# A gated delta-net kernel on one core: one 64x64 Gram product per unit, the first group inverted on VectorE, a new order by chunk

## The chip, the core and the metric

The kernel runs on one NeuronCore of a Trainium2 chip. The metric is device microseconds of one execution; the kernel before was run three times, and the median counts. TensorE (PE) multiplies, VectorE (DVE), ScalarE (ACT) and GpSimd (POOL) work element by element, and SyncE (SP) issues the DMAs. [...]

## The reference

Four batches with 8 heads each hold 768 tokens of 48 features, in float32. The first part is a recurrence over the tokens, the second a gated convolution on its output.

```python
def _attn_ref(q, k, v, beta):
    k_n = k / (np.linalg.norm(k, axis=-1, keepdims=True) + 1e-06)
    state = np.zeros((B, H, D, D))
    for t in range(S):
        y[:, :, t] = np.einsum('bhd,bhde->bhe', q[:, :, t], state)
        v_old = np.einsum('bhde,bhd->bhe', state, kt)
        state = state + bt[:, :, :, None] * np.einsum('bhd,bhe->bhde', kt, vt - v_old)

def _moe_ref(x, w_val, conv_w, w_out):      # x: the four batches, 768 tokens, 384 features
    for k in range(5): gate_pre += conv_w[k] * xp[:, k:k + S, :]
    gate = 1.0 / (1.0 + np.exp(-gate_pre))
    return (gate * (x @ w_val)) @ w_out
```

## The kernel before

The tokens are cut into 12 chunks of 64, two chunks to a group, and each chunk is done for all 32 pairs of batch and head at once. Only the state goes from chunk to chunk.

For a **group**, `prep` makes the inverse of a triangular matrix for each of its 64 units (a pair of batch and head in a chunk; 64 tokens, cut into two blocks of T=32). `gram` multiplies the keys with keys and queries: per head four streams (two row halves by two column halves of the array), and in each two products of 32 rows, with a moving operand of up to 96 columns. Its PSUM result is copied by ACT into GD (`gk`: per row block the diagonal 32x32 block and the lower left one) and multiplied by a mask on DVE into AQ (`ga`). DVE then transposes the diagonal blocks so that units lie on partitions (`trans_in` into TLP), takes norms and coefficients (`coef`), and inverts: 8x8 blocks row by row (`row`), pairs of them to 16x16 (`mergez8`, `merget8`). From there two ways lead on. Group 0 (`FAST`) packs the 16x16 inverses, transposes them back and builds the 32x32 inverses on PE with `p1`, `p2`, `p3` and ACT copies. All other groups go on on DVE with `zmul`, `zred`, `tmul`, `tred`, and transpose the result twice, into BD (`trans_t`) and into TNA (`trans_n`). Last, `lev1` and `lev2` on PE with ACT copies (`zevac`, `tevac`) put the off-diagonal 32x32 block into BD.

For a **chunk**, `chain` does `estep` (keys by state) and `esum`, `qstep`, `ustep` (inverse times ES, the chunk's update), `sstep` (new state, accumulated in the PSUM banks SPS) and `ystep` (output); `flip` transposes the output into X. `moe` follows: `halo` carries the last four tokens over, `conv` does the first `nt` of the five taps of the convolution on PE, `tap` the others on DVE, then `sig`, `val`, `gate`, `outp` and the output's DMA. The taps on PE are 2 in chunks 0 to 5 and 1 in chunks 6 to 11 (`TAPS`, `PTAP`).

The two 384x384 weights and the convolution's come as float64 and are made float32 by five steps of ACT and DVE (`f64_bits`), one of ACT (`f64_low`) and two of POOL (`f64_join`), over two staging buffers that are the tiles GT and OS.

What sets the order: all operations are added to a `Plan` with an engine, an estimated cost and their inputs and outputs. The plan gives each a rank (the length of what follows it, plus a number of the table `BIAS` by kind and group), and lays them out greedily by estimated time. Six PSUM banks are handed out on the way. Where it thinks PE idle or little used it puts in `keep_warm`, a product of zeros (128x128 by 128) into an unused part of SPS. The result is a fixed list for each engine. Loads go through SP in the plan's order, each behind a one-element DMA (PACE) that reads what the load two before it has written, so that two are in flight.

Of the kernel before, what the change touches and what calls it, by code (L numbers as in the profile page):

```python
# [21 lines left out]
KW = 5 * T  # L22
# [3 lines left out]
NBANK = 6  # L26
BIAS = {
    'LB': -1138.3, ('LB', 0): 7.4, 'LK0': 530.9, ('LK0', 0): -481.0, 'LKQ': 1110.0, ('LKQ', 0): -19.7,
    ('LKQ', 1): 156.3, ('LKQ', 2): 217.7, ('LKQ', 3): -442.9, ('LKQ', 4): -892.6, ('LKQ', 5): -89.1, 'LKT': -576.7,
    ('LKT', 0): -196.1, ('LKT', 1): -334.4, ('LKT', 2): 445.2, ('LKT', 3): -254.0, ('LKT', 4): 323.2,  # L30
# [30 lines left out]
    ('outp', 0): -290.2, ('outp', 1): -378.5, ('outp', 2): 246.7, ('outp', 3): 155.7, ('outp', 4): 185.1,
    ('outp', 5): 238.1, 'p1': -8.9, ('p1', 0): -189.4, 'p2': -61.8, 'p2evac': -59.9, ('p2evac', 0): 440.8,
    ('p2', 0): -32.9, 'p3': 33.8, 'p3evac': 482.3, ('p3evac', 0): 751.7, ('p3', 0): -185.1, 'pack': -348.7,
    ('pack', 0): 465.1, 'qstep': 59.2, ('qstep', 0): 391.9, ('qstep', 1): 424.1, ('qstep', 2): -186.8,
    ('qstep', 3): -217.3, ('qstep', 4): -80.2, ('qstep', 5): -107.5, 'row': -870.9, ('row', 0): 33.6,
# [948 lines left out]
```

## Time and profile before

| | |
|---|---|
| three runs | 342.68, 342.65, 339.18 us; median 342.65 |
| profiled execution | 342.16 us, of which the program's span is 340.4 |
| PE busy | 294.2 us (86%) in 8370 matmuls |
| DVE busy | 265.4 us (78%) in 655 instructions |
| ACT, POOL busy | 195.9 us (58%), 17.6 us (5%) |
| DMA | 34.58 MB, 102 GB/s over the span |

A float32 product of the program is two matmuls in the profile, each with its own weight load; transposes are one. [...] The chain of waits gives PE 45% of the span, DVE 21%, ACT 15%, and 10% to "issue", time in which an engine waited for nothing that the profile shows. The profile begins with setup and the first groups' inversions, and the first `ustep` starts at 66.66 us; from about 110 us on PE is busy nearly throughout.

### The profile page before, as it was taken

The page shows a single profiled execution, that of the slowest core. Times are in us where ns is not written, and L with a number is a line of the kernel's source. Part 1 is how long each engine was busy: PE and PEld are TensorE (multiplying, and loading weights), DVE is VectorE, ACT ScalarE, POOL GpSimd, SP SyncE. Part 2 cuts the span into 40 slices and gives each one's busy share as a digit, 9 for nine tenths or more (in the row PEclk, how much of TensorE's full clock was granted, in tenths as well). Part 3 has the DMA queues.
Part 4 walks back from the last instruction along what each step waited for, and adds up shares of the span by engine and source line. Part 5 has one row for each costly group of instructions (what it writes and reads, how often), then busy time and mean ns, then how long its engine had stood idle before and what let it go on. Part 6 is the DMA issues. An engine that isn't in the chain of part 4 may idle for free.

```text
span 340.4 us, 18482 instructions
## 1 busy us (share of the span) xinstructions
PE 294.2 (86%) x8370; PEld 236.6 (70%) x8370; DVE 265.4 (78%) x655; ACT 195.9 (58%) x569; POOL 17.6 (5%) x31
## 2 busy tenths in 40 slices
PE   5898544977859898988996997998999999999994
PEld 4797544876647776875875885877866787687862
DVE  5569869895257999998999866999999899827430
ACT  4211759999545965357955478616599351873321
POOL 0000022322200000000000000000000000000000
PEclk9589855969678999999999589999999999999999
DMA  4885666131612527060147104345221301300213
GB/s 149 271 251 155 193 187 187 52 91 58 202 53 81 171 54 233 19 196 11 50 81 257 58 4 157 62 125 162 58 65 26 98 4 25 73 4 2 49 23 69
DMA packets 12379, 34.58 MB, mean 102 GB/s; under 512 B 1933, under 2 KB 5133, under 8 KB 12301
## 3 DMA queue, kind: packets, MB, share of 16 engines
q1 hardware_dynamic: 12300, 33.41, 33.4%
q8 instruction: 65, 1.06, 1.3%
q14 instruction: 14, 0.11, 0.1%
HBM read 28.69 MB, written 4.72 MB: 98 GB/s over the span
## 4 chain that ended last, share of the span: by engine, by line
PE 45%; DVE 21%; ACT 15%; issue 10%; DMA 7%; SPq 0%; POOL 0%; DVEq 0%; ACTq 0%
PE PB L907 8%; PE SPS L958 6%; PE PB L915 5%; PE PB L892 5%; ACT VN L348 5%; PE PB L484 5%; DMA KQ<-in_kq_dram 5%; DVE GT L898 4%; PE PB L801 2%; ACT BD L348 2%; PE PB L833 2%; DVE ZT L606 2%; ACT US L348 2%; DVE PR L599 2%; PE PB L851 2%
## 5 line engine op out<-in xcount | busy, mean ns | idle before, releaser
L907 PE MATMUL PB<-X,WV 128*128 128x256 f32 x216 | 52.5, 388 | 1.5 <-DVE GT L910 1.0
L915 PE MATMUL PB<-WO,GT 128*128 128x384 f32 x144 | 50.6, 495 | 0.1
L348 ACT ACTIVATE VN<-VN,NRM 128x48 f32<-128x48 f32 x192 | 45.1, 326 | 2.2 <-DMA PACE<-VN 2.0
L907 PEld LDWEIGHTS PB<-X,WV 128*128 128x128 f32 x216 | 39.8, 191 | 8.5 <-DVE GT L910 1.2
L898 DVE SCALAR_TENSOR_TENSOR GT<-X,CW,GT 128x256 f32<-128x256 f32 x90 | 38.7, 478 | 0.1
L958 PE MATMUL SPS<-ZW 128*128 128x128 f32 x214 | 35.1, 319 | 3.0 <-DVE SPS L400 2.8
L915 PEld LDWEIGHTS PB<-WO,GT 128*128 128x128 f32 x144 | 26.3, 190 | 15.5 <-DVE GT L910 0.3
L484 PE MATMUL PB<-KQ 48*32 48x96 f32 (+2 forms) x1536 | 26.6, 263 | 11.7 <-issue 9.2
L958 PEld LDWEIGHTS SPS<-ZW 128*128 128x128 f32 x214 | 31.2, 224 | 4.4 <-DVE SPS L400 2.8
L484 PEld LDWEIGHTS PB<-KQ 48*32 48x32 f32 x1536 | 21.3, 113 | 16.0 <-issue 11.9
L892 PE MATMUL PB<-X,CD 128*128 128x256 f32 x108 | 32.0, 432 | 0.1
L348 ACT ACTIVATE OS<-PB 128x384 f32<-128x384 f32 x24 | 11.6, 487 | 34.4 <-PE PB L915 33.1
L910 DVE TENSOR_TENSOR GT<-PB,GT 128x256 f32<-128x256 f32 x36 | 14.9, 417 | 20.5 <-PE PB L907 20.5
L494 DVE TENSOR_TENSOR AQ<-PB,MASK 128x256 f32<-128x256 f32 x48 | 19.2, 418 | 12.7 <-ACT GD L348 12.6
L898 DVE SCALAR_TENSOR_TENSOR GT<-X,CW,PB 128x256 f32<-128x256 f32 x36 | 16.6, 475 | 13.8 <-PE PB L892 8.7
L348 ACT ACTIVATE US<-PB 64x384 f32<-64x384 f32 (+1 forms) x36 | 17.5, 486 | 16.8 <-PE PB L812 9.2
L348 ACT ACTIVATE GD<-PB 128x256 f32<-128x256 f32 x48 | 15.6, 381 | 18.8 <-PE PB L484 18.4
L348 ACT ACTIVATE BD<-PB 32x256 f32<-32x256 f32 (+1 forms) x50 | 19.1, 383 | 8.7 <-PE PB L697 5.8
L892 PEld LDWEIGHTS PB<-X,CD 128*128 128x128 f32 x108 | 21.0, 210 | 3.6 <-DVE GT L898 0.3
L902 ACT ACTIVATE GT<-GT 128x256 f32<-128x256 f32 x36 | 13.6, 413 | 15.3 <-DVE GT L898 15.2
L841 PEld LDWEIGHTS PB<-US,AQ 64*64 64x64 f32 x768 | 14.3, 146 | 9.7 <-ACT US L348 7.1
L348 ACT ACTIVATE ZS<-PB 32x256 f32<-32x256 f32 x48 | 17.9, 373 | 4.1 <-PE PB L686 3.1
(117 smaller groups left out, 481.9 us busy)
## 6 DMA issues: line engine op xcount, KB each, us to landing
KQ<-in_kq_dram SPq DMA_DIRECT2D x24, 640.0 KB, 5.0
VN<-in_vt_dram SPq DMA_DIRECT2D x12, 384.0 KB, 3.5
KT<-in_kt_dram SPq DMA_DIRECT2D x12, 384.0 KB, 3.2
out_dram<-OS SPq DMA_DIRECT2D x48, 96.0 KB, 2.2
BD<-in_k_dram SPq DMA_DIRECT2D x2, 512.0 KB
OS<-in_w_val_dram SPq DMA_DIRECT2D x2, 384.0 KB, 4.0
GT<-in_w_out_dram SPq DMA_DIRECT2D x2, 384.0 KB
PACE<-KQ SPq DMA_DIRECT2D x24, 0.0 KB
```

The source lines that it names most:

```text
L348: A.activation(out=out, in_=in_, func=AF.Copy, **kw)
L484: PE.matmul(o, w, y, start=True, stop=True, tile_position=(64 * r, q))
L494: V.tensor_tensor(out=AQ[c % NAQ][:, r, 4 * i:4 * i + 4, :].rearrange("p h (n t) -> p h n t", t=T), in0=gview(c, i, r, part)[:, :, 0:3:2, ...
L599: V.tensor_tensor(out=PR[:, 0:64 * n].rearrange("p (k i j) -> p k i j", k=4, i=16), op=ALU.mult, in0=tl4[:, 1, :, 0, 4 * kb:16].unsqueeze( ...
L841: PE.matmul(bank("y", c, r)[a:a + C, D * h:D * h + D], aq[64 * t:64 * t + C, r, h, :], us[64 * t:64 * t + C, r, h, :], start=c == 0 and h ...
L892: PE.matmul(p, CD[:, m, k], x[:, m, :, k:k + C], start=(k == 0), stop=(k == nt - 1))
L898: V.scalar_tensor_tensor(out=GT[m], in0=x[:, m, :, k:k + C], scalar=CW[:, m, k:k + 1], in1=csum(m) if k == nt else GT[m], op0=ALU.mult, op ...
L902: A.activation(out=GT[m], in_=csum(m) if nt == KS else GT[m], func=AF.Sigmoid)
L907: PE.matmul(p, WV[:, k, 128 * m:128 * m + 128], xs[:, k], start=(k == 0), stop=(k == NKX - 1))
L910: V.tensor_tensor(out=GT[m], in0=bank("v", c, m)[:, 0:B * C].rearrange("p (b t) -> p b t", t=C), in1=GT[m], op=ALU.mult)
L915: PE.matmul(bank("o", c, i)[:, 0:DM], GT[k][:, 2 * i:2 * i + 2, :].rearrange("p b t -> p (b t)"), WO[:, k, :], start=(k == 0), stop=(k == ...
L958: PE.matmul(SPS[0][:, 384:512], ZW, ZW, start=False, stop=True, skip_group_check=True)
```

## The change

- `FAST` and its functions are gone (`pack`, `trans_x`, `split`, `p1`, `wsum`, `p2`, `p2evac`, `p3`, `p3evac`, and the constants they need): group 0 takes the way of the others on DVE.
- `gram` does one product per stream and head: 64 stationary columns, and 128 moving columns (64 for group 0, whose keys alone come first from K0). The queries no longer stand twice in the load, so a KQ load has 128x1024 elements, not 128x1280. The blocks of the result lie otherwise: a new `place`, two ACT copies of 32 partitions by 1024 elements per group, brings the two upper diagonal blocks to where `trans_in` reads them.
- TNA is laid out [128, T, NU]: `trans_n` writes it contiguously, and `lev2` reads its stationary operand with a stride of 32 elements.
- `halo` runs on ACT instead of POOL.
- The taps on PE are 3 in chunks 0 to 5 (2 before); chunks 6 to 11 keep 1.
- `BIAS` is a new table, by chunk where it was by group (`plan.part = c`), and the planner's costs and columns are changed; with them the lists of all engines. The program's products on PE: `gram` 896 before and 448 now, `p1` to `p3` 320 and 0, `conv` 54 and 72, `keep_warm` 107 and 181; the others as before.

```diff
-KW = 5 * T
+KW = 4 * T
...
-FAST = (0,)
-TAPS = 2
-PTAP = {6: 1, 7: 1, 8: 1, 9: 1, 10: 1, 11: 1}
+TAPS = 3
+PTAP = {2: 3, 6: 1, 7: 1, 8: 1, 9: 1, 10: 1, 11: 1}
...
-TICK_COLS = 1450.0
+TICK_COLS = 1270.0
...
-    TNA = sb.tile([128, NU, T], F32, name="TNA")
+    TNA = sb.tile([128, T, NU], F32, name="TNA")
...
     def gram(c, i, part):
-        x = KQ[c % NKQ]
-        for j in range(4):
-            h = 4 * i + j
-            for k in range(2):
-                for r, t in STREAMS:
-                    q = 64 * t + 32 * k
-                    o = bank("g", c, i, r, part)[q:q + 32, 96 * j:96 * j + 96].rearrange("p (n t) -> p n t", t=T)
-                    if part == "K":
-                        y = K0[64 * r:64 * r + D, c, t ^ r, h, :]
-                        w, y = y[:, k * T:k * T + T], y.rearrange("p (n t) -> p n t", t=T)
-                        y, o = y if k else y[:, 0:1].to_broadcast([D, 2, T]), o[:, 0:2, :]
-                    else:
-                        y = x[64 * r:64 * r + D, t ^ r, h, :]
-                        w, y = y[:, (2 + k) * T:(3 + k) * T], y.rearrange("p (n t) -> p n t", t=T)
-                        n, m = {"": ((0, 5, 2), (0, 3, 1)), "Q": ((0, 5, 4), (0, 3, 2))}[part] if k == 0 else \
-                            {"": ((2, 5, 1), (0, 3, 1)), "Q": ((4, 5, 1), (2, 3, 1))}[part]
-                        y, o = y[:, n[0]:n[1]:n[2], :], o[:, m[0]:m[1]:m[2], :]
-                    PE.matmul(o, w, y, start=True, stop=True, tile_position=(64 * r, q))
-
-    def gview(*key):
-        return bank("g", *key)[:, 0:384].rearrange("p (h n t) -> p h n t", n=3, t=T)
+        for h in range(4 * i, 4 * i + 4):
+            for r, t in STREAMS:
+                y = (K0[:, c] if part == "K" else KQ[c % NKQ])[64 * r:64 * r + D, t ^ r, h, :]
+                n = y.shape[-1] if part == "" else C
+                PE.matmul(bank("g", c, i, r, part)[64 * t:64 * t + C, n * (h % 4):n * (h % 4) + n], y[:, 0:C],
+                          y[:, C:] if part == "Q" else y, start=True, stop=True, tile_position=(64 * r, 64 * t))
+
+    def gview(c, i, r, part):
+        n = C if part else 2 * C
+        return bank("g", c, i, r, part)[:, 0:4 * n].rearrange("p (h n) -> p h n", n=n)
 
     def gk(c, i, r, part):
         u = 16 * (c % 2) + 8 * r + 4 * i
-        copy(GD[c // 2 % 2][:, u:u + 4, :].rearrange("p h (n t) -> p h n t", t=T), gview(c, i, r, part)[:, :, 0:2, :])
+        copy(GD[c // 2 % 2][:, u:u + 4, :], gview(c, i, r, part)[:, :, 0:C])
 
     def ga(c, i, r, part):
-        V.tensor_tensor(out=AQ[c % NAQ][:, r, 4 * i:4 * i + 4, :].rearrange("p h (n t) -> p h n t", t=T),
-                        in0=gview(c, i, r, part)[:, :, 0:3:2, :], op=ALU.mult,
-                        in1=MASK.rearrange("p (n t) -> p n t", t=T).unsqueeze(1).to_broadcast([128, 4, 2, T]))
+        V.tensor_tensor(out=AQ[c % NAQ][:, r, 4 * i:4 * i + 4, :], in0=gview(c, i, r, part)[:, :, 0 if part else C:],
+                        in1=MASK.unsqueeze(1).to_broadcast([128, 4, C]), op=ALU.mult)
...
+        def place(q):
+            copy(GD[gb][q:q + 32, :, T:], GD[gb][q:q + 32, :, 0:T])
...
-            V.transpose(out=TNA.rearrange("p u k -> p k u"), in_=tf)
...
+            V.transpose(out=TNA, in_=tf)
...
-                    PE.matmul(bank("o2", g, i)[to:to + 32, T * j:T * j + T], TNA[q:q + 32, 16 * i + j, :], ZS[i][q:q + 32, j, :],
+                    PE.matmul(bank("o2", g, i)[to:to + 32, T * j:T * j + T], TNA[q:q + 32, :, 16 * i + j], ZS[i][q:q + 32, j, :],
...
+            plan.part = c
             loads(c)
             plan_gram(c, "Q" if g == 0 else "")
         for c in (2 * g, 2 * g + 1):
+            plan.part = c
             tokens(c)
...
-        add("DVE", 1.87, trans_in, r=GDT[0] + GDT[1], w=["TL"])
+        for q in (0, 64):
+            add("ACT", 1.05, place, (q,), r=GDT[0] + GDT[1], w=[("GDp", gb, q)])
+        add("DVE", 1.87, trans_in, r=GDT[0] + GDT[1] + [("GDp", gb, q) for q in (0, 64)], w=["TL"])
...
-        if g in FAST:
-            for b in range(2):
-                add("ACT", 0.5, pack, (b,), r=["TT"], w=["PR"])
-            add("DVE", 0.63, trans_x, w=["PR"])
-            add("ACT", 1.15, split, (1,), r=["PR", "MHI"], w=["RH"])
-            add("ACT", 1.15, split, (0,), r=["PR", "TRQ"], w=["TZ"])
-            for i in range(2):
-                add("PE", 1.1, p1, (i,), cols=512, size=256, r=["RH"] + GDT[i], w=[("wp", i)], take=[("w", g, i)])
...
-            add("DVE", 1.87, trans_n, r=["TT"] + tm, w=[("TNA", i, q) for i in range(2) for q in (0, 64)])
...
+        add("DVE", 1.2, trans_n, r=["TT"] + tm, w=[("TNA", i, q) for i in range(2) for q in (0, 64)])
...
-            G.tensor_copy(out=XB[(c + 1) % 3][:, :, :, 0:4], in_=x[:, :, :, C:C + 4])
+            copy(XB[(c + 1) % NXB][:, :, :, 0:4], x[:, :, :, C:C + 4])
...
-            add("POOL", 0.3, halo, r=X_, w=[("Xh", (c + 1) % 3)])
+            add("ACT", 0.25, halo, r=X_, w=[("Xh", (c + 1) % NXB)])
...
-    kq = rows(_np.stack([fq[0], fq[1], fk[0], fk[1], fq[1]], axis=-2))
+    kq = rows(_np.stack([fk[0], fk[1], fq[0], fq[1]], axis=-2))
```

Three places show how the lists moved.

**SP, the first loads** (KQ_61 to KQ_64 are the keys and queries of chunks 0 to 3, BD_83 the buffer that holds K0, VN and KT the values and keys by token). Before:

```order
L353 DMA BD_83<-in_k_dram 128x1024 x2
L353 DMA BE<-in_beta_dram 128x192
L360 DMA PACE<-GD_71 1x1
L363 DMA KQ_63<-in_kq_dram 128x1280 x2
L358 DMA PACE<-KQ_63 1x1
L363 DMA KQ_64<-in_kq_dram 128x1280
L358 DMA PACE<-KQ_63 1x1
L363 DMA KQ_64<-in_kq_dram 128x1280
L358 DMA PACE<-KQ_64 1x1
L363 DMA KQ_62<-in_kq_dram 128x1280
L358 DMA PACE<-KQ_64 1x1
L363 DMA KQ_62<-in_kq_dram 128x1280
```

Now:

```order
L375 DMA KT_65<-in_kt_dram 128x768
L375 DMA VN_70<-in_vt_dram 128x768
L370 DMA PACE<-KT_65 1x1
L375 DMA VN_68<-in_vt_dram 128x768
L370 DMA PACE<-VN_70 1x1
L375 DMA VN_69<-in_vt_dram 128x768
L370 DMA PACE<-VN_68 1x1
L375 DMA KT_66<-in_kt_dram 128x768
L370 DMA PACE<-VN_69 1x1
L375 DMA GT<-in_conv_w_dram 128x30
L370 DMA PACE<-KT_66 1x1
L375 DMA OS<-in_w_val_dram 128x768
```

The values and keys by token, the convolution's weights and the first block of w_val now stand ahead of all KQ loads, and chunk 1 is the first of these, followed by chunks 2 and 3, with chunk 0 after them.

**PE, between the keys' Gram of group 0 (from BD_83) and the first one from a KQ load.** Before:

```order
L484 MATMUL PB_126<-BD_83 32x64
L484 MATMUL PB_127<-BD_83 32x64
L958 MATMUL SPS_124<-ZW 128x128 x5
L484 MATMUL PB_128<-KQ_63 32x96
L484 MATMUL PB_129<-KQ_63 32x96
```

Now:

```order
L473 MATMUL PB_121<-BD_83 64x64
L473 MATMUL PB_122<-BD_83 64x64
L894 MATMUL SPS_119<-ZW 128x128 x93
L473 MATMUL PB_123<-KQ_62 64x64
L473 MATMUL PB_124<-KQ_62 64x64
```

Five `keep_warm` became 93. Before the first `ustep` there were 78 of them and there are 156; from there to the `ustep` of chunk 2 there were 3 and there are 20; after that 26 and 5. Counted through the two lists, products of the program in the stretch from the first `ustep` to chunk 2's: `conv` 10 before and 18 now, `val` 0 and 15, `outp` 0 and 6, calls of `gram` (four heads each) 4 and 4, `lev1` and `lev2` together 160 and 128, the chain's five steps two each, `flip` 12. From chunk 2's `ustep` to the end: `val` 108 and 93, `outp` 72 and 66, `conv` 44 and 54, calls of `gram` 12 and 12, all others equal.

**ACT, ahead of the first `ustep`'s copies (US_87).** ZS is written by `zevac`, BD_82 from PB by `tevac`, WV and WO by `f64_low`, GT and OS from themselves by the first step of `f64_bits`. Before:

```order
L348 ACTIVATE ZS_84<-PB_126 32x8x32 x4
L437 ACTIVATE WV<-OS 128x384
L348 ACTIVATE ZS_85<-PB_127 32x8x32 x2
L348 ACTIVATE BD_82<-PB_128 32x8x32 x4
L425 ACTIVATE GT<-GT 128x384
L348 ACTIVATE ZS_85<-PB_127 32x8x32 x2
L348 ACTIVATE VN_70<-VN_70,NRM_108 128x48 x8
L348 ACTIVATE US_87<-PB_129 128x384
```

Now:

```order
L360 ACTIVATE ZS_84<-PB_123 32x8x32 x4
L360 ACTIVATE ZS_85<-PB_124 32x8x32 x3
L439 ACTIVATE WV<-OS 128x384
L360 ACTIVATE ZS_85<-PB_124 32x8x32
L427 ACTIVATE GT<-GT 128x384
L439 ACTIVATE WO<-GT 128x384
L360 ACTIVATE BD_82<-PB_123 32x8x32 x4
L360 ACTIVATE BD_82<-PB_125 32x8x32 x4
L360 ACTIVATE VN_70<-VN_70,NRM_105 128x48 x8
L360 ACTIVATE US_87<-PB_126 128x384
```

The copies into BD_82 that the first `ustep` reads stand behind the conversion of a block of w_out, which waits for DVE's fourth `f64_bits` step on it; that step stands in DVE's list behind group 0's `trans_n` and group 1's `trans_in`.

## Rows read from the trace of the kernel before

**Rows 1.** The page: its span, and PE's granted clock in 40 slices.

```profile
span 340.4 us, 18482 instructions
...
PEclk9589855969678999999999589999999999999999
```

**Rows 2.** Windows: stretch, length, busy PE, PEld, DVE, ACT, POOL, then clock, DMA, GB/s.

```profile
66.66:109.85 43.19, 34.06 (x1255) 28.70 (x1255) 25.57 (x59) 30.67 (x86) 7.35 (x9) 0.76 0.31 93
109.85:335.66 225.81, 213.17 (x5361) 165.02 (x5360) 188.16 (x432) 129.98 (x381) 2.77 (x9) 0.98 0.28 80
9.93:32.15 22.22, 21.13 (x576) 19.17 (x579) 17.03 (x58) 3.15 (x10) 0.00 (x0) 0.77 0.72 221
187.00:197.00 10.00, 9.71 (x228) 8.49 (x228) 7.58 (x13) 5.14 (x13) 0.22 (x1) 0.52 0.19 58
```

**Rows 3.** Timeline of PE: start, duration, line, instruction, idle time ahead of it.

```profile
4.13 3.05 PE L484 MATMUL PB<-BD 48*32 48x64 f32 x219
8.63 0.63 PE L484 MATMUL PB<-BD 48*32 48x64 f32 x37 [1.45 <-issue]
...
21.11 1.86 PE L484 MATMUL PB<-KQ 48*32 48x96 f32 x128
22.90 3.17 PE L958 MATMUL SPS<-ZW 128*128 128x128 f32 x26
...
57.43 0.63 PE L671 MATMUL PB<-TZ,WS 32*32 32x32 f32 x27 [2.35 <-issue]
...
66.66 1.61 PE L812 MATMUL PB<-VN,BD 64*64 64x48 f32 x64
```

**Rows 4.** The same later on: chunk 2's ustep and the last matmuls.

```profile
109.85 1.15 PE L812 MATMUL PB<-ES,BD 64*64 64x48 f32 x64
...
334.10 1.56 PE L915 MATMUL PB<-WO,GT 128*128 128x384 f32 x4
```

**Rows 5.** PE's waits after chunk 2's ustep began: in total, times, longest.

```profile
PE PB L484 <- issue: 4.0, 3, 1.4
```

**Rows 6.** Chain of waits where PE follows PE: start, us, what.

```profile
305.56 1.49 PE PB L892 x6
307.05 1.08 PE PB L801 x64
308.13 2.79 PE PB L907 x12
...
312.00 2.13 PE PB L915 x6
```

**Rows 7.** Timeline of DVE: trans_in of group 0, trans_x, trans_n of group 1.

```profile
9.93 1.91 DVE L523 STREAM_TRANSPOSE TLP<-GD 128x1024 f32<-128x1024 f32 x1 [3.24 <-ACT GD L348]
...
34.87 0.67 DVE L635 STREAM_TRANSPOSE PR<-PR 128x512 f32<-128x512 f32 x1
...
72.22 1.96 DVE L626 STREAM_TRANSPOSE TNA<-TT__78 128x1024 f32<-128x1024 f32 x1
```

**Rows 8.** Groups of DVE by line: count, busy us in total, mean ns.

```profile
L898 DVE SCALAR_TENSOR_TENSOR GT<-X,CW,GT 128x256 f32<-128x256 f32 x90 | 38.7, 478 | 0.1
L494 DVE TENSOR_TENSOR AQ<-PB,MASK 128x256 f32<-128x256 f32 x48 | 19.2, 418 | 12.7 <-ACT GD L348 12.6
L599 DVE TENSOR_TENSOR PR<-TLP,TT__78 128x1024 f32<-128x1024 f32 (+3 forms) x20 | 17.0, 851 | 0.3
...
L619 DVE TENSOR_REDUCE TT__78<-PR 128x64 f32<-128x256 f32 (+3 forms) x20 | 16.3, 814 | 0.3
...
L431 DVE SCALAR_TENSOR_TENSOR OS<-OS 128x384 uint32<-128x384 uint32 x3 | 1.7, 555 | 0.0
```

**Rows 9.** Timeline of ACT ahead of the first ustep.

```profile
59.66 0.72 ACT L348 ACTIVATE BD<-BD,M 128x512 f32<-128x512 f32 x1
...
65.62 1.57 ACT L348 ACTIVATE BD<-PB 32x256 f32<-32x256 f32 x4
```

**Rows 10.** DMA queues: packets, MB, share of 16 engines' span.

```profile
q8 instruction: 65, 1.06, 1.3%
```

More of the change, by code (lines that the diff above doesn't have):

```diff
@@ L61 @@
[L61 to L65, printed above, removed]
@@ L408 @@
     add("DVE", 0.8, mask, r=["TRQ"], w=["MASK"])
-    add("DVE", 0.4, small, (EQ, EYE), r=["EYE"], w=["EQ"])
-    add("DVE", 0.1, high, r=["TRQ"], w=["MHI"])
     add("DVE", 1.0, zero, (TT_,), w=["TT"])
     add("DVE", 0.1, zero, (XB[0][:, :, :, 0:4],), w=[("Xh", 0)])
-    add("ACT", 0.6, const, (WS[:, :, 0:16], EQ[:, 0:16]), r=["EQ"], w=["WSc"])
-    add("ACT", 0.6, const, (TZ[:, :, 16:32], EQ[:, 16:32]), r=["EQ"], w=["TZc"])
     def f64_parts(n, i):
@@ L711, in plan_gram @@
             use = [("K0", c)] if part == "K" else [("KQ", c % NKQ, a) for a in range(2)]
-            cost, cols = {"": (0.9, 939), "K": (0.7, 626), "Q": (0.7, 626)}[part]
+            cost, cols = {"": (0.88, 768), "K": (0.5, 384), "Q": (0.5, 384)}[part]
             for i in range(2):
                 gg = [("g", c, i, r, part) for r in range(2)]
-                add("PE", cost, gram, (c, i, part), cols=cols, size=128, r=use, w=[("gp", c, i, r, part) for r in range(2)],
+                add("PE", cost, gram, (c, i, part), cols=cols, size=64, r=use, w=[("gp", c, i, r, part) for r in range(2)],
                     take=gg, kind="gram" + part)
@@ L719, in plan_gram @@
                     if part != "Q":
-                        add("ACT", 0.35, gk, (c, i, r, part), r=tok, w=[("GD", gb, c % 2, i, r)],
+                        add("ACT", 0.36, gk, (c, i, r, part), r=tok, w=[("GD", gb, c % 2, i, r)],
                             give=gg[r:r + 1] if part else ())
@@ new lines, in prep @@
+        add("ACT", 0.65, turn, (16,), r=["TT"], w=["TR"])
+        for kb in range(4):
+            add("DVE", 0.06 + 64 * (16 - 4 * kb) / 960.0, zmul, (kb,), r=["TL", "TT"], w=["PR"])
+            add("DVE", 0.07 + 64 * (16 - 4 * kb) / 960.0, zred, (kb,), r=["PR"], w=["ZT"])
+        for ib in range(4):
+            add("DVE", 0.06 + 64 * (4 + 4 * ib) / 960.0, tmul, (ib,), r=["ZT", "TR"], w=["PR"])
+            add("DVE", 0.07 + 64 * (4 + 4 * ib) / 960.0, tred, (ib,), r=["PR"], w=[("TTm", ib)])
@@ L776, in prep @@
+        tm = [("TTm", i) for i in range(4)]
+        add("DVE", 2.15, trans_t, r=["TT"] + tm, w=[("BD", gb, i, z) for i in range(2) for z in ("H",) ] + k0_free)
+        add("DVE", 1.2, trans_n, r=["TT"] + tm, w=[("TNA", i, q) for i in range(2) for q in (0, 64)])
         for i in range(2):
-            add("ACT", 0.55, bd0, (i,), r=[("BD", gb, i, "H"), "MASK"], w=[("BD", gb, i, "L")])
-            add("PE", 0.75, lev1, (i,), cols=256, size=128, r=GDT[i] + [("BD", gb, i, "H")], w=[("z", i)], take=[("z", g, i)])
+            add("ACT", 0.62, bd0, (i,), r=[("BD", gb, i, "H"), "MASK"], w=[("BD", gb, i, "L")])
+            add("PE", 0.74, lev1, (i,), cols=128, size=128, r=GDT[i] + [("BD", gb, i, "H")], w=[("z", i)], take=[("z", g, i)])
@@ L787, in prep @@
             for r in range(2):
-                add("ACT", 1.4, vscale, (c, r), r=[("NRM", gb)], w=[("VN", c % NKT, r)])
+                add("ACT", 1.83, vscale, (c, r), r=[("NRM", gb)], w=[("VN", c % NKT, r)])
     def chain(c):
@@ L858, in chain @@
         if c:
-            add("PE", 1.05, estep, cols=938, size=128, r=KQr + Sr, w=both("ep"), take=both("e"))
+            add("PE", 1.05, estep, cols=576, size=128, r=KQr + Sr, w=both("ep"), take=both("e"))
             for r in range(2):
@@ L862, in chain @@
         if c:
-            add("PE", 1.08, qstep, cols=938, size=128, r=KQr + Sr, w=both("yp") + ["q"], take=both("y"))
-        add("PE", 1.05, ustep, cols=1086, size=128, w=both("up"), take=both("u"),
+            add("PE", 1.05, qstep, cols=576, size=128, r=KQr + Sr, w=both("yp") + ["q"], take=both("y"))
+        add("PE", 1.1, ustep, cols=768, size=128, w=both("up"), take=both("u"),
             r=([("ES", r) for r in range(2)] if c else [("VN", c % NKT, r) for r in range(2)])
@@ L953 @@
         for c in (2 * g, 2 * g + 1):
+            plan.part = c
             chain(c)
```

266 lines of the change are left out of this document (113 added, 153 removed), and 26 rows, old and new, of the table BIAS.

## The prediction

> **What bounds the kernel now.** I read the page first, then windows, then PE's timeline, its waits and the chain. The page gives a span of 340.4 us, and a clock that is at full speed nearly throughout the second half and often at half of it in the first [rows 1]. So I cut the span where the character changes: at the first `ustep`, which starts at 66.66 us [rows 3], and at chunk 2's, which starts at 109.85 [rows 4].
>
> The stretch up to 66.66 is a chain through DVE, then PE and ACT: group 0's `trans_in` starts at 9.93 [rows 7], the last piece of `p3` starts at 57.43 after an idle 2.35 us that nothing but "issue" explains [rows 3]. Between 66.66 and 109.85 PE is busy 34.1 of 43.2 us at a mean clock of 0.76, DVE only 25.6 [rows 2]. After that PE is busy 213.2 of 225.8 us at 0.98, DVE 188.2 [rows 2]: this is PE's stretch, and its last matmul ends at 334.10 + 1.56 = 335.7 [rows 4], 4.7 us ahead of the span's end.
>
> **PE's prices.** Where PE follows PE [rows 6], three products of `conv` take 1.49 us (0.50 each), a chain step 1.08, six of `val` 2.79 (0.465 each), three of `outp` 2.13 (0.71 each). Two calls of `gram` take 1.86 (0.93 each) and 13 `keep_warm` 3.17 (0.244 each) [rows 3].
>
> **The stretch after chunk 2's `ustep`.** The other list has 15 `val` less (-7.0 us), 6 `outp` less (-4.3), 21 `keep_warm` less (-5.1) and 10 `conv` more (+5.0), because the earlier stretch took the work over and three taps are on PE: **-11.4 us**.
>
> `gram`: 12 calls here either way. A call had 64 matmuls with up to 96 columns and has 32 with 128. By instructions alone it would halve, to 0.47 us. By columns for each place in the array (64x96/8 = 768 before, 32x128/4 = 1024 now) it would rise to 0.93 x 4/3 = 1.24. The chain step is the nearest row, with the same 64-row tiles: 64 matmuls of 48 columns, 768 for each place, in 1.08 [rows 6]; it is bounded by both. I take 1.0: **+1 us** for 12 calls, -5.5 to +3.7. [...]
>
> Losses: PE has 225.8 us there. By the old list and these prices it works 208: `val` 50.2, `outp` 51.1, `conv` 21.9, `gram` 11.2, 47 chain steps 50.8, `keep_warm` 6.3, and some 17 for `lev1`, `lev2` and `flip`. So about 18 are lost. Of this, 4.0 are three "issue" waits inside `gram` [rows 5], and some 5 are the ten microseconds at clock 0.52 after 187 us, in which PE was busy 9.71 us [rows 2]. What "issue" is shows at the very start: PE stops for 1.45 us in the middle of the keys' Gram, after 219 of its 256 matmuls [rows 3], with no semaphore in sight; and one DMA queue moves 1.06 MB of instructions [rows 10], 63 bytes for each of the 2 x 8370. PE outran its program there. Gram with half the instructions needs half the supply, so I take three quarters of the 4.0 back, and half of the 5 lost to the clock, since that slow stretch follows such stops: 3 + 2.5, **-6 us** rounded. Bounds: 0, and -9 if both go whole. [...]
>
> The strided weight read of `lev2` is in no row. Its 12 calls keep their number, and each has as many matmuls as a chain step, 1.08 us at most [rows 6]; between no cost and a doubling lie 13 us. I take none, since the next call's weights load beside running matmuls, and keep 4 in the range.
>
> **Up to the first `ustep`.** K0 is issued behind the small beta load and its Gram has half the instructions, so the 1.45 us stop goes; two `place` copies of 1024 elements come in (512 take 0.72 us on ACT [rows 9], so between 0.7 and 1.4 each; I take 1.1). These cancel, and `trans_in` starts at 10 us as before. DVE then works without a gap: its first part was busy 17.0 us in 22.2, 12 AQ products among them [rows 2]; without these (0.40 each [rows 8]) it is 12.2, with the small gaps between dependent operations 13. The second part is four groups like L599 to L619, (17.0 + 16.4 + 16.4 + 16.3)/5 = 13.2 for a group [rows 8]. The 12 AQ add 4.8, 19 steps of weight conversion some 6 (0.57 us the dearest of them [rows 8]), the BD transpose 2.0, `trans_n` contiguous 1.3 (twice the 0.67 of the 512-wide one, not 1.96 [rows 7]): 10 + 13 + 13.2 + 4.8 + 6 + 2 + 1.3 = 50. Now ACT's list matters. The copies into BD stand behind a conversion that needs DVE's fourth step on w_out; ahead of that come group 1's `trans_in` (1.9), four AQ (1.6), nine `coef` (1.8) and five conversion steps (2): 57.6. Conversion and four copies take 0.6 and 1.57 [rows 9]. So the first `ustep` starts at about **60**, not 66.7. ACT's removed copies of `pack` to `p3evac` lie off this path.
>
> **To chunk 2's `ustep`.** By the other list PE has 18 `conv` (9.0), 15 `val` (7.0), 6 `outp` (4.3), 4 `gram` (4.0), ten chain steps (10.5), `lev` and `flip` (some 4), 20 `keep_warm` (4.9): 43.6 us. DVE, from 57.6 on, has the rest of group 1's inversion (11 and 13.2), 12 taps (0.43 each [rows 8], 5.2), 12 AQ, `esum` and `gate` (some 6), eight conversion steps (3), a BD transpose, group 2's `trans_in` and first `coef` (5.6): 44. They come out alike, 103.6 and 101.6, so either waits on the other a little: **105**, from 101 to 114 (as many waits as before). `halo` on ACT, eleven copies, and the six groups' `place` hide there: ACT is idle for 96 of the last 226 us [rows 2]. Without that cover they would cost a chain the 2.2 us of `place` per group. The fifth that each KQ load loses frees the DMA queue, which hides under DVE.
>
> **Sum.** 340.4 - (109.9 - 105) - 11.4 + 1 - 6 = 319.1; the profiled execution took 1.8 us more than its span, so **321 us**. That execution, 342.16, stands 0.5 below the median of the three runs.
>
> **Rivals.**
> - Supply and clock come back whole (-9 where I took -6), `gram` is bound less by columns than I think (0.7 us a call, -4), and DVE keeps pace (101 where I took 105): 310 us. For it: the 4.0 us of waits stand in `gram` itself. Against it: three things at once. Chance 0.20.
> - The two engines wait on each other in the early stretch, or the 93 `keep_warm` ahead of chunk 1's Gram run at half clock as PE did around 10 to 20 us before [rows 1]. At full clock they end at 7.2 + 22.7 = 30, about when DVE asks for that Gram; 10 us at half clock make it 35, and DVE stands 4 us. With chunk 2 at 114: 330 us. Chance 0.18.
> - The clock falls later. Only 5 `keep_warm` of 26 remain after chunk 2's `ustep`, and each stop of PE can be followed by a stretch like that at 187 us, 10 us at half clock, 5 lost [rows 2]. From five such stretches on, one for every two chunks, it is 321 + 25 = 346: slower. Against it: the clock held from 198 us to the end, with few stops [rows 1]. Chance 0.07.
> - The lists are only reshuffled: DVE, busy 188 of 226 us before [rows 2] and with the same work in less time now, makes PE wait for the 11 us that were moved ahead, and the early 5 are lost with them: 337 to 342, no change. Chance 0.05.
>
> **Numbers.** The forecast has 0.50. The range reaches from 307 (the first rival and a little) to 338 (the second, with the strided read and dear `gram`). About 1% can be told from no change here: faster than 339.2 has 0.87, within 1% 0.06, slower 0.07.
>
> **What would show it.** First `ustep` at 57 to 63 us, its ACT copies into BD straight behind a WO conversion; chunk 2's at 101 to 114. `gram` in 32 matmuls of 0.9 to 1.1 us a call, "issue" waits after chunk 2 under 4 us in all. Clock above 0.97 after 110 us. `trans_n` at 1.3 us, `lev2` no longer than before. The prediction is wrong if the early stretch loses more than 15 us to waits, or if PE's busy share after chunk 2's `ustep` falls below 0.9.

## The result, and the profile after

The change made the kernel faster: **316.97 us** median (315.28 to 319.21, 4 runs) against 340.91 (335.95 to 342.68, 4 runs of before beside them), a ratio of 0.939 (95% interval 0.926 to 0.953). The forecast was 321, its range 307 to 338. The profiled execution took 315.92 us with a span of 314.2.

The page of the kernel after, to be held against [rows 1] and [rows 10] of before (PEclk is the granted clock in tenths of full speed):

```profile
span 314.2 us, 15755 instructions
...
PE 296.1 (94%) x7018; PEld 244.7 (78%) x7018; DVE 267.3 (85%) x647; ACT 206.3 (66%) x580; POOL 15.1 (5%) x20
...
PEclk9999997899999999999999999999999999999999
...
q8 instruction: 55, 0.90, 1.2%
```

PE's busy time over the whole span hardly moved (294.2 us before, 296.1 now), so the 26 us came out of its idle time. The windows of the three stretches of after (columns as in [rows 2]: length, then PE, PEld, DVE, ACT and POOL busy, PEclk, DMA):

```profile
0.00:61.70 61.70, 54.06 (x953) 51.39 (x953) 50.87 (x136) 32.85 (x92) 10.44 (x16) 0.94 0.57 176
61.70:108.28 46.58, 44.26 (x1156) 37.16 (x1155) 45.17 (x120) 34.93 (x97) 4.66 (x5) 1.00 0.35 104
108.28:309.30 201.02, 197.80 (x4913) 156.15 (x4912) 171.23 (x393) 138.12 (x393) 0.00 (x0) 1.00 0.27 76
```

Chunk 2's `ustep` came only 1.6 us earlier, the stretch behind it shrank by 24.8. In that stretch PE was idle for 12.6 us before and is idle for 3.2 now, and the clock is full (1.00, 0.98 before). PE's groups by line there, after (busy, mean ns of one | idle before):

```profile
L847 PE MATMUL PB<-WO,GT 128*128 128x384 f32 x133 | 47.1, 496 | 0.0
L839 PE MATMUL PB<-X,WV 128*128 128x256 f32 x186 | 44.7, 387 | 0.1
L824 PE MATMUL PB<-X,CD 128*128 128x256 f32 x108 | 28.1, 394 | 0.1
L473 PE MATMUL PB<-KQ 48*64 48x128 f32 x384 | 12.7, 273 | 0.5 <-issue 0.5
...
L639 PE MATMUL PB<-ZS,TNA 32*32 32x32 f32 x512 | 9.8, 224 | 0.3 <-DVE ROOT L531 0.3
```

and the same of before, those that differ most:

```profile
L907 PE MATMUL PB<-X,WV 128*128 128x256 f32 x216 | 52.5, 388 | 1.5 <-DVE GT L910 1.0 <-DVE AQ L494 0.3
...
L484 PE MATMUL PB<-KQ 48*32 48x96 f32 x768 | 12.9, 252 | 5.3 <-issue 4.0 <-DMA KQ<-in_kq_dram 1.3
...
L697 PE MATMUL PB<-ZS,TNA 32*32 32x32 f32 x512 | 6.3, 194 | 1.3 <-issue 1.3
```

Busy and idle together, `val` gave 9.2 us, `outp` 3.6, `keep_warm` 7.0, `gram` 5.0 (4.8 of it idle), the chain steps, `lev1` and `flip` some 6; `conv` took 3.4 more and `lev2` 2.5: its matmuls grew from 194 to 224 ns.

**What "issue" is.** PE's timeline of before, the stops around `p1` to `p3` (start, duration, in brackets the idle time ahead); the fourth, at 57.43, is in [rows 3]:

```profile
44.50 0.56 PE L646 MATMUL PB<-RH,GD 32*32 32x16 f32 x26 [4.92 <-issue]
48.88 1.93 PE L659 MATMUL PB<-WS,TZ 32*32 32x32 f32 x128 [2.45 <-issue]
53.15 0.49 PE L659 MATMUL PB<-WS,TZ 32*32 32x32 f32 x20 [2.35 <-issue]
```

They end 4.3 to 4.4 us apart. The 65 packets of [rows 10] for 2 x 8370 matmuls and weight loads are 257 instructions each, and after it is 55 packets for 2 x 7018, 255 each. By the timeline's counts, the stops that end at 8.63, 34.58, 44.50, 48.88 and 53.15 us stand behind 446, 1722, 2234, 2490 and 2746 matmuls and weight loads of PE: the first 190 past a multiple of 256, the others 186. The small drift comes from semaphore instructions on PE's list, which the timeline does not print. Counted with these, which the trace holds, every issue stop of before (20) and of after (7) stands 193 or 194 past a multiple of 256, and so do all 117 of the fourteen profiled executions here.

So PE stands at the ends of 256-instruction pieces of its program, and the trace's DMA records show what it waits for: each of the 27 stops of before and after ends 1.24 to 1.57 us behind the landing of a packet of the instruction queue, 16384 bytes. Two such packets never start less than 3.40 us apart in before and 3.30 in after.

After, the one long stop is of this kind too, behind 1466 matmuls and weight loads, 186 past a multiple:

```profile
47.66 1.30 PE L628 MATMUL PB<-BD,GD 32*32 32x32 f32 x128 [0.58 <-DVE BD L616]
48.89 0.82 PE L894 MATMUL SPS<-ZW 128*128 128x128 f32 x5
52.37 0.37 PE L894 MATMUL SPS<-ZW 128*128 128x128 f32 x1 [2.65 <-issue]
52.67 1.99 PE L473 MATMUL PB<-KQ 48*64 48x64 f32 x64
54.58 2.93 PE L894 MATMUL SPS<-ZW 128*128 128x128 f32 x12
57.44 1.22 PE L639 MATMUL PB<-ZS,TNA 32*32 32x32 f32 x64
...
61.70 1.57 PE L741 MATMUL PB<-VN,BD 64*64 64x48 f32 x64
```

So where PE ran through its pieces quickly, the next came some 4.3 us behind the last. And the long stop had an echo: from 51.3 us, inside the stop, to 58.1 us the granted clock was 0.50. In before it fell to 0.50 six times ahead of PE's end, at 9.83, 40.55, 71.27, 84.92, 98.58 and 187.32 us, each time inside an issue stop or at most 2.13 us behind the end of one.

### The profile page after: what moved, and what is told of

The parts are those of the page before. It is cut to its first block, busy times and chain, and to the rows that moved or that the text cites. A ratio compares the mean times of both kernels' runs of the same rounds, so it can differ in the third digit from the quotient of the medians.

```text
span 314.2 us, 15755 instructions
## 1 busy us (share of the span) xinstructions
PE 296.1 (94%) x7018; PEld 244.7 (78%) x7018; DVE 267.3 (85%) x647; ACT 206.3 (66%) x580; POOL 15.1 (5%) x20
## 4 chain that ended last, share of the span: by engine, by line
PE 62%; DVE 29%; issue 3%; DMA 2%; ACT 1%; SPq 0%; DVEq 0%; ACTq 0%
PE PB L839 12%; PE PB L847 11%; PE PB L824 11%; PE PB L473 6%; PE PB L639 4%; PE PB L741 4%; PE PB L770 3%; PE PB L730 3%; DVE PR L605 3%; PE PB L762 3%; DVE TT__78 L612 3%; PE SPS L751 2%; DVE GT L830 2%; DVE BD L616 2%; PE PB L628 2%
## 5 line engine op out<-in xcount | busy, mean ns | idle before, releaser
L894 PE MATMUL SPS<-ZW 128*128 128x128 f32 x362 | 47.5, 289 | 5.5 <-DVE SPS L406 2.8
L360 ACT ACTIVATE VN<-VN,NRM 128x48 f32<-128x48 f32 x192 | 45.2, 323 | 7.4 <-DVE NRM L545 7.4
L894 PEld LDWEIGHTS SPS<-ZW 128*128 128x128 f32 x362 | 44.4, 201 | 4.3 <-DVE SPS L406 2.8
L847 PEld LDWEIGHTS PB<-WO,GT 128*128 128x128 f32 x144 | 26.2, 190 | 15.2 <-issue 0.2
L824 PE MATMUL PB<-X,CD 128*128 128x256 f32 x144 | 36.6, 391 | 0.1
L830 DVE SCALAR_TENSOR_TENSOR GT<-X,CW,GT 128x256 f32<-128x256 f32 x72 | 32.6, 478 | 0.1
L473 PEld LDWEIGHTS PB<-KQ 48*64 48x64 f32 x768 | 20.8, 141 | 6.7 <-DVE TLP L516 3.0
L473 PE MATMUL PB<-KQ 48*64 48x128 f32 (+1 forms) x768 | 24.5, 272 | 1.2 <-DMA KQ<-in_kq_dram 0.7
L360 ACT ACTIVATE BD<-PB 32x256 f32<-32x256 f32 x48 | 18.0, 374 | 8.4 <-PE PB L639 6.0
L605 DVE TENSOR_TENSOR PR<-ZT,TR 128x256 f32<-128x256 f32 (+3 forms) x24 | 20.6, 857 | 0.1
L592 DVE TENSOR_TENSOR PR<-TLP,TT__78 128x1024 f32<-128x1024 f32 (+3 forms) x24 | 19.6, 816 | 0.1
L599 DVE TENSOR_REDUCE ZT<-PR 128x64 f32<-128x1024 f32 (+3 forms) x24 | 19.4, 810 | 0.2
```

The source lines that it names most:

```text
L360: A.activation(out=out, in_=in_, func=AF.Copy, **kw)
L473: PE.matmul(bank("g", c, i, r, part)[64 * t:64 * t + C, n * (h % 4):n * (h % 4) + n], y[:, 0:C], y[:, C:] if part == "Q" else y, start=Tru ...
L592: V.tensor_tensor(out=PR[:, 0:64 * n].rearrange("p (k i j) -> p k i j", k=4, i=16), op=ALU.mult, in0=tl4[:, 1, :, 0, 4 * kb:16].unsqueeze( ...
L599: V.tensor_reduce(out=z16[:, 4 * kb:4 * kb + 4, :], axis=AX.X, op=ALU.add, in_=PR[:, 0:64 * n].rearrange("p (k i j) -> p k i j", k=4, i=16))
L605: V.tensor_tensor(out=PR[:, 0:64 * n].rearrange("p (k i j) -> p k i j", k=16, i=4), op=ALU.mult, in0=z16[:, :, 0:n].unsqueeze(2).to_broadc ...
L824: PE.matmul(p, CD[:, m, k], x[:, m, :, k:k + C], start=(k == 0), stop=(k == nt - 1))
```

## The experiments

Unless it says otherwise, an experiment is the changed kernel with every engine's list in the same order. One kernel's runs mostly scatter by 1 to 2%, so differences under 3 us between variants are not called differences.

**Gram and order, crossed.** The old Gram in the new order:

```
-            PE.matmul(bank(..)[64*t:64*t+C, n*(h%4):..], y[:, 0:C], y, ..)           # 64x64, 128 columns
+            PE.matmul(bank(..)[q:q+32, 96*j:..], y[:, (2+k)*T:(3+k)*T], pieces, ..)   # 32 rows, to 96 columns, twice as many
```

> The changed kernel in its own order, with the Gram of before (32-row pieces, up to 96 columns each, twice the matmuls; the place copies are left out, since the old form writes both copies itself). Theory: PE's instruction supply is what the new Gram relieves: the sum of issue waits goes from 5 back to above 12 us, most of it in or just behind the Gram, Gram's own busy time stays within 10%, and the time rises to 324 to 330 us. Rival: the new order alone made the gain: issue stays under 7 us and the time within 2 us of 317.

326.68 us (324.92 to 330.25), 0.962 of before (0.951 to 0.973): the theory's time, and the issue waits rose to 15.2 us. But only 5.3 us of them stood in the Gram itself; the others stood wherever else a piece ended. And the new Gram in the old order, in the kernel before:

> The kernel before in its own order, with only the new Gram (one 64x64 product a unit, the query and key block of 4T columns, the two place copies ahead of each trans_in). Theory: the issue waits of 10.7 us in the Gram mostly go, those at p1 to p3 stay or shift: 330 to 335 us instead of 341. Rival: the stops only move to the next dense stretch of matmuls and the place copies cost DVE's chain 2 us a group where it is late: 338 to 342.

342.64 us (341.14 to 347.96), 1.010 (1.000 to 1.021): just above the rival's band, by another way than it said. The stretches of the profiled executions, and PE's waits in its timeline:

| order, Gram | first ustep | chunk 2's ustep | from there to PE's end | issue / other waits | median |
|---|---|---|---|---|---|
| old, old | 66.7 | 109.8 | 225.8 | 29.5 / 10.7 | 340.9 |
| old, new | 65.3 | 109.6 | 225.0 | 10.8 / 29.7 | 342.6 |
| new, old | 69.6 | 116.8 | 206.9 | 15.2 / 5.0 | 326.7 |
| new, new | 61.7 | 108.3 | 200.9 | 4.8 / 7.5 | 317.0 |

("New order" holds the inversion on DVE and the taps on PE too. The third row's execution was its longest, 330.25.) The new Gram took 19 us of issue away in the old order and got nothing for it: as many microseconds of other waits came up in their place. PE's longest waits in that kernel:

```profile
PE PB L649 <- issue: 4.8, 2, 2.5
PE PB L636 <- ACT RH L348: 4.6, 1, 4.6
PE PB L831 <- ACT US L348: 3.6, 6, 1.1
PE PB L471 <- DMA KQ<-in_kq_dram: 2.9, 3, 1.4
PE SPS L948 <- DVE SPS L400: 2.8, 1, 2.8
PE PB L882 <- DVE SQ L517: 2.8, 1, 2.8
PE PB L823 <- ACT ST L348: 2.7, 2, 2.1
```

Waits for ACT alone rose from 4.4 to 16.0 us there. ACT also had the twelve `place` copies, put where `trans_in` stood in the old order; whether these or the order itself ate the gain, no run separates. In the new order the same edit is worth 9.7 us by the medians, and 7.6 by the ratios to before beside each run (0.962 and 0.939). So 14 of the 24 us came with the new order and the other operations even under the old Gram, and the last 8 to 10 needed the new Gram in an order made for it.

**Half a piece of shift**, which moves only the ends of the 256-instruction pieces:

```
-        keep_warm()
+        if seen <= 3 or seen > 35: keep_warm()
```

> The changed kernel without 32 of the 93 keep_warm products that follow the keys' Gram (nothing waits for them). In the traces each issue stop of the early stretch stands at the same place of a 256-instruction piece of PE's program. 32 products are 128 instructions, half a piece, so everything behind is half a piece earlier. Theory (PE waits for the next piece of its program): the 2.65 us stop at 52.4 us, behind group 0's lev1, goes or falls under 1.2 us, the clock does not fall behind it, the first ustep starts at 58 to 60 instead of 61.7; other stops appear half a piece off, in all under 6 us; time 313 to 318. Rival 1: the stop is a wait for DVE, ACT or a DMA that the profile misses: it stays at 52 us with 2 us or more. Rival 2: the seven idle microseconds ahead of chunk 1's Gram cost the clock, and the time is 319 or more.

319.92 us (317.01 to 322.49): the time missed the theory's range and lies in rival 2's. But the stop moved as the theory said, and the first ustep started at 58.70:

```profile
50.35 1.14 PE L473 MATMUL PB<-KQ 48*64 48x64 f32 x59 [0.26 <-DMA KQ<-in_kq_dram]
52.72 0.27 PE L473 MATMUL PB<-KQ 48*64 48x64 f32 x1 [1.22 <-issue]
52.91 1.61 PE L894 MATMUL SPS<-ZW 128*128 128x128 f32 x12
54.45 1.22 PE L639 MATMUL PB<-ZS,TNA 32*32 32x32 f32 x64
...
215.54 0.55 PE L730 MATMUL PB<-ST,KQ 48*64 48x48 f32 x17 [1.74 <-issue]
```

That settles what the stop is, and rival 1 falls. Rival 2's slow clock came (0.51 from 28 to 35 us), yet the first `ustep` was early all the same, so it is not what cost the time up to there. The three microseconds reached nobody: ACT's copies of `US` stood behind a `vscale` that waits for DVE, and chunk 2's `ustep` came at 108.0. Behind it two new stops came, of 1.74 us ahead of 215.54 and 1.54 ahead of 225.52, each with a slow clock after it (0.66 from 215 to 220 us and from 225 to 230); that stretch took 206.4 us instead of 200.9:

```profile
210.00:215.00 5.00, 3.80 (x180) 3.19 (x178) 4.99 (x8) 1.85 (x5) 0.00 (x0) 1.00 0.68 194
215.00:220.00 5.00, 4.46 (x83) 4.04 (x87) 3.23 (x4) 1.74 (x5) 0.00 (x0) 0.66 0.03 8
```

**The strided weight read.**

```
-    TNA = sb.tile([128, T, NU], ..)      -  V.transpose(out=TNA, in_=tf)
+    TNA = sb.tile([128, NU, T], ..)      +  V.transpose(out=TNA.rearrange("p u k -> p k u"), in_=tf)
```

> The changed kernel in its own order, but the inverse lies unit by unit again: trans_n writes with a stride (1.96 us as before, instead of 1.23), lev2 reads its weights contiguously. Theory: the strided weight read is what made lev2 longer (225 ns a matmul record instead of 194, some 0.45 us a call, 12 calls), and PE, which bounds the kernel from the first ustep on, pays it: lev2 falls back to 194 ns, and the time to about 313 us, since 5.4 us leave PE and the 0.7 x 6 added on DVE are mostly hidden. Rival 1: DVE's 4.4 us eat it, 317. Rival 2: lev2 was longer for its new place in the order and not for the stride: still 225 ns, and 317 to 321 us.

317.53 us (315.95 to 318.67): rival 1's time. All twelve calls of `lev2`, after, and in this kernel:

```profile
L639 PE MATMUL PB<-ZS,TNA 32*32 32x32 f32 x768 | 14.5, 225 | 0.3 <-DVE ROOT L531 0.3
```
```profile
L639 PE MATMUL PB<-ZS,TNA 32*32 32x32 f32 x768 | 9.7, 198 | 1.3 <-DVE QUOT L527 0.6 <-DVE ROOT L531 0.5 <-issue 0.2
```

So the stride costs PE 4.8 us, 0.4 a call, and saving it buys nothing that can be measured: chunk 2's `ustep` came 0.7 us earlier, the stretch behind it took 203.4 instead of 200.9, with 4.7 us of issue in it instead of 1.9. It may be that PE reaches the ends of its pieces sooner; DVE has `trans_n` longer (1.96 us where it wrote with a stride in before, 1.23 in after).

**The fillers.**

```
-        keep_warm()
+        if seen <= 143: keep_warm()          # none behind 54.6 us
```

> The changed kernel without the 38 keep_warm products that stand behind group 0's first Gram on the queries (from 54.6 us on), the 143 ahead of it kept. Theory: they only fill, and 12 of them stand ahead of the first lev2 whose operands are there at 53.5: the first ustep starts near 59 instead of 61.7, the clock stays at full speed as PE has few stops, and the time is 314 to 317 us. Rival: the granted clock falls to half in the stretch from 54 to 78 us, where PE now stands still in places, and the time is 319 to 324 us.

326.02 us (318.57 to 330.66); the four runs lie too far apart for a ratio, and the fastest is within 2 us of the changed kernel's median, so it stays open whether the kernel is slower. In the profiled execution (325.58) the first `ustep` came at 58.4, as the theory said, yet the clock was 0.50 from there to 72 us, and chunk 2's `ustep` came at 109.9. Later too a stop had its echo:

```profile
144.66 0.57 PE L639 MATMUL PB<-ZS,TNA 32*32 32x32 f32 x22
147.52 0.87 PE L639 MATMUL PB<-ZS,TNA 32*32 32x32 f32 x42 [2.29 <-issue]
148.32 2.82 PE L839 MATMUL PB<-X,WV 128*128 128x256 f32 x6
```

Six matmuls of `val` took 2.82 us behind that stop and 1.56 ahead of it. The rival's slow clock came in that execution, but it does not say for which reason: 38 fillers are 152 instructions, so the ends of all later pieces moved as well, and behind chunk 2's `ustep` issue was 7.0 us instead of 1.9.

**Which engine bounds.** The third tap of chunks 2 to 5 back on DVE:

```
-            for k in range(nt): PE.matmul(p, CD[:, m, k], ..)
+            for k in range(nt - 1): PE.matmul(..)      # and one tap more on DVE
```

> The changed kernel in its own order, with the third convolution tap of chunks 2 to 5 taken from PE back to DVE: 12 conv products less on PE (0.48 us each, 5.8 us), 12 taps of 0.45 us more on DVE (5.4 us). Theory: between chunk 2's ustep and 260 us DVE is as full as PE (98% and 99% in the 30 us stretches), so what PE gives up, DVE must take, and the time is 317 to 322. Rival: PE alone bounds that stretch, and the time is 311 to 314.

322.87 us (320.38 to 328.02): slower, and just above the theory's range; the profiled execution, its longest, has 7.1 us of other waits behind chunk 2's `ustep` where there were 0.7. DVE is as full as PE there, as the theory had it (28.1, 26.8, 28.8 and 29.6 us busy in the four 30 us stretches from 112.5 us on, PE 27.2 to 28.3). The reverse, the last `conv` products of the late chunks as ACT copies, for chunks 10 and 11, and for 6 to 11:

```
-            if not nt: copy(GT[m], x[:, m, :, 0:C], scale=CW[:, m, 0:1])
+            if not nt or c in (10, 11): copy(..)
```

> The changed kernel in its own order, with the one conv product that PE still does for chunks 10 and 11 (six products, 0.48 us each) replaced by six scaled copies on ACT (some 0.4 us each). From 260 us on PE is busy 97 to 100% and DVE 37 to 63%, ACT 26 to 58%. Theory: PE alone bounds that end, and the time falls by 2 to 3 us, to 314 or 315. Rival: chunk 11's part lies on the chain from its last flip through ACT and DVE to its val and outp, where a copy in ACT's queue is no shorter than the product: no change or 1 us slower.

> The changed kernel in its own order, with the one conv product that PE still does for chunks 6 to 11 (18 products of 0.48 us, 8.6 us) replaced by 18 scaled copies on ACT (some 0.4 us). Theory: for chunks 10 and 11 this gave 3.2 us; for 6 to 9 DVE is as full as PE (29.3 to 29.4 of 30 us), so little comes on top: 312 to 315. Rival 1: PE alone bounds the stretch: 308 to 310. Rival 2: PE reaches the ends of its 256-instruction pieces sooner, stops there for over a microsecond and the clock falls behind: 317 or more.

313.76 us (312.82 to 316.34) and 316.69 (313.28 to 318.25). For 6 to 11, 5 us left PE's busy time (291.2) and 8.4 us of waits for others stood behind chunk 2's `ustep`: rival 1 is out. The theory's 312 to 315 was missed too, and not by rival 2's way, with 1.1 us of issue there.

**All operations, old numbers.** The planner of after with the table of before:

> All operations of the changed kernel, but the planner has the old table of numbers (by group) and so writes another order: chunk 2's ustep stands behind 12 conv and no val or outp where the new order has 18, 15 and 6, and there are 267 keep_warm instead of 181. Theory: the operations are worth little without an order that fits them: 328 to 338 us. Rival: the operations alone make the gain: within 4 us of 317.

371.04 us (367.86 to 375.81), 1.089 of before (1.081 to 1.097). The direction is the theory's, the size is far beyond it: the old numbers were found for other operations and costs, so this does not price the order by itself. It shows that the operations bring no gain in an order that does not fit them.

**Towards a better kernel.** The early stretch mended:

```
+ 32 nudge() (32x32 zero products) ahead of the 93 keep_warm, 32 behind the first ustep
- 28 keep_warm from 54.6 to 66.8 us       + 28 nudge() in their places
- ACT: VN (vscale), US, TR, US, US        + ACT: US, US, US, VN, TR
```

> The changed kernel with its early stretch mended in three places: 32 small zero products (32x32, 128 instructions) ahead of the 93 keep_warm, and 32 behind the first ustep, so that PE's program lies half a 256-instruction piece later in between and as it was behind; the 28 keep_warm from 54.6 to 66.8 us become such small products one for one; on ACT the first chunk's three US copies go ahead of group 1's first vscale and turn, which wait for DVE. Theory: the stop at 52.4 us and DVE's 1.65 us wait behind it go, the first ustep starts at 57 to 59, its sstep follows at once instead of 7 us later, and chunk 2's ustep comes at 105 to 107 instead of 108.3, DVE being busy 45 of the 46.6 us before it; the later stretch stays at 201: 313 to 316 us. Rival: DVE alone sets chunk 2's ustep and the later stretch takes back what is won, as in the kernels with the contiguous lev2 and with half a piece of shift: 317 to 320.

317.05 us (313.01 to 318.81): first `ustep` at 57.7, chunk 2's at 107.0 as the theory had it, and no gain in the median. Here the pieces behind the first `ustep` lie as in the changed kernel, and the stretch from chunk 2's `ustep` on took 199.2 us with 1.4 of issue, where the shift alone made it 206.4 with 4.2: once more, it seems, the place of the pieces' ends, though two other edits stand beside it. The early stretch still held a stop, 1.50 us inside `lev2`, and the 47 small products behind the first `ustep` took 5.2 us at a clock of 0.50:

```profile
56.77 0.50 PE L639 MATMUL PB<-ZS,TNA 32*32 32x32 f32 x17 [1.50 <-issue]
...
57.69 1.96 PE L741 MATMUL PB<-VN,BD 64*64 64x48 f32 x64
59.58 5.21 PE L897 MATMUL SPS<-ZW 32*32 32x32 f32 x94
64.72 1.53 PE L751 MATMUL SPS<-US,KT 64*48 64x48 f32 x64
```

Last, this and the ACT copies for chunks 10 and 11 together, beside the changed kernel itself on the same chip:

> Two edits in one: the mended early stretch (half a piece of shift, small products for 28 keep_warm, the US copies ahead of vscale) and the ACT copies in place of the last conv product of chunks 10 and 11. Theory: the two lie in different stretches, so they add: chunk 2's ustep at 107, the stretch behind it 197 instead of 201, and 312 to 314 us, 3 to 5 below the changed kernel run beside it. Rival: the early gain does not reach the end, and it is as with the copies alone, 314 to 315, or no better than the changed kernel.

> The changed kernel as it is, on the same chip as the kernel with both mends, so that the two can be compared: 316 to 318 us, as when it was first seen (315.3 to 319.2).

314.92 us (313.92 to 316.67) and 314.32 (313.50 to 317.02), 0.929 and 0.928 of before. The two edits give nothing that can be measured. In its profiled execution the stretch behind chunk 2's `ustep` was 197.5 us against 199.1, but that `ustep` came at 110.5 against 108.3: the fillers ahead of chunk 1's Gram, with the 32 small ones (3.6 us), ran to 36.2 us instead of 31.3, and DVE stood 3.9 us for that Gram. Since the changed kernel itself came out at 314.3 here, the 313.8 of the copies alone is no gain shown either. **No version beat it.**

## Why the prediction was right, and where not

The time came 4 us below the forecast partly by luck, because two errors went opposite ways: up to chunk 2's `ustep` the change gave 1.6 us where 4.9 were forecast, and behind it 24.8 where 16.4 were.

- **Moved work, -11.4.** The counts by line came as listed: `val` 216 to 186 matmuls, `conv` 89 records to 108, `keep_warm` 52 to 10. At the predicted prices that is the -11.4; the rows give -16.4 since before's also held stops and slow clock, which the prediction had under losses.
- **Losses, -6: the mis-sized term.** The stretch lost 24.8 us. Less the moved work (11.4), less 0.2 that `gram` got cheaper in busy time, plus 3.5 that `lev2` got dearer, losses gave back 16.7, nearly all of the 18 that the prediction counted, and beyond its bound of -9. It took three quarters of the stops in `gram` alone and half of one slow stretch. The rest was put at nothing and went as well: issue outside `gram` fell from 2.7 to 1.4 us, waits for other engines and the DMA from 5.0 to 0.7, and the clock rose from 0.98 to 1.00. The waits for others were down to 0.4 us already with the old Gram in the new order, so they went with the order and the other operations. With the old Gram (in its longest execution) 6.0 us of issue were left there at a clock of 0.98, and the stretch was 6.0 us longer: a stop can cost twice, itself and the clock behind it.
- **`gram` at 1.0 us a call.** Right: two calls in 1.98 us where they took 1.86, and busy 12.9 before and 12.7 after for twelve. Neither bound held. By columns for each place alone it would have risen by a third, to 1.24; that was the author's estimate, and no run shows it: a call went from 0.93 to 0.99.
- **`lev2` at no cost: wrong.** 4.8 us in all. Only eight of the twelve calls lie behind chunk 2's `ustep`, where the prediction counted all; there it was 3.5, nearly the kept 4. The contiguous read shows that as things stand it decides nothing measurable.
- **`trans_in` at 10: 11.92.** The term "these cancel" failed: the keys' Gram waited 0.9 us for its DMA and ended only 0.2 us sooner, and two `place` copies took 2.12. `trans_n` took 1.23 and ended at 50.4, where 50 was said, so DVE's work took 38.5 us instead of the 40 summed.
- **First `ustep` at 60: 61.7, by another path.** The claim on ACT's queue failed: the conversion that it named ran at 53.9, and the copies into BD waited 4.31 us for `lev2`, which stood behind the 2.65 us stop, the Gram and six fillers at half clock.

```profile
11.92 1.97 DVE L516 STREAM_TRANSPOSE TLP<-GD 128x1024 f32<-128x1024 f32 x1 [5.83 <-ACT GD L360]
...
53.85 0.76 DVE L485 TENSOR_TENSOR AQ<-PB,MASK 128x256 f32<-128x256 f32 x2 [1.65 <-PE PB L473]
```
```profile
58.78 1.57 ACT L360 ACTIVATE BD<-PB 32x256 f32<-32x256 f32 x4 [4.31 <-PE PB L639]
```

- **Chunk 2's `ustep` at 105: 108.3.** Both engines alike, as said (PE busy 44.3 of 46.6 us, DVE 45.2); the first ustep's delay and DVE's 1.65 us wait for that same Gram came on top.
- **The supply of instructions.** The stops were there and fell, as the prediction said: 29.5 us of them before and 4.8 after, each ending 1.24 to 1.57 us behind the landing of a packet. A packet holds 255 to 257 instructions by the counts, and a stop moved with the shift of half a piece.
- **Rivals.** Supply and clock coming back whole was the nearer mechanism, without its cheap `gram` and early chunk 2, and the time fell between it and the forecast. The second rival's wait did not come: the 93 fillers ended at 30.6 us at full clock (1.00). The clock did not fall late for want of fillers (1.00 behind 108 us with five of them). DVE did not hold PE back by what was moved ahead, so the reshuffle without gain fell too.

Why two instruction packets start at least 3.40 us apart in before and 3.30 in after stays open. So does the worth of the order by itself, of the inversion on DVE, of the third tap in chunks 0 and 1 and of the halo on ACT; no run took them alone (the halo's copies took 0.24 us each).

## What to carry to other kernels

Count where a kernel's issue stops stand in 256-instruction pieces before trusting a price per operation: here a form with half the instructions was worth nothing in the order where other waits took the place of the stops, and 8 to 10 us in the order made for it. Where PE, DVE and the program's supply lie close together, as here, a microsecond taken from one alone can come back as a wait for the next: none of the single edits to the changed kernel shortened it measurably. Cost a long stop with the slow clock that may follow: here 2.65 us, and 0.50 of the clock for 6.8 us from inside it on.

## Not expected of the hardware

- Packets of 255 to 257 PE instructions, 16384 bytes each, never started less than 3.40 us apart in before and 3.30 in after, and each stop of PE for one ended 1.24 to 1.57 us behind its landing. Four stops in a row ended 4.3 to 4.4 us apart (44.50, 48.88, 53.15, 57.43 us).
- Falls of the granted clock to 0.50 stood at stops: inside the 2.65 us one of the changed kernel, at six in before, and the clock was 0.57 and 0.64 in the first 2 us behind the 1.74 and 1.54 us ones of the half-piece shift. Not every stop had one: before's stops of 1.45 us ahead of 118.96 and 1.32 ahead of 136.20 left it at 1.00. What decides stays open.
- Reading 32x32 weights with a stride of 128 bytes, `lev2`'s matmuls took 225 ns each instead of 198, and 14.5 us busy for 768 instead of 9.7.
